# VectorE's share of a two-problem attention kernel: shifted exponential terms made for four key blocks at once, with re-gated weight loads and spread exponentials

## The chip, the cores and the metric

The kernel runs on one core of a Trainium2 chip. The metric is the device time in microseconds (us) of one execution, inputs in HBM to outputs in HBM. The core's engines run side by side, each with its own instruction stream in a fixed order: TensorE (PE), VectorE (DVE), ScalarE (ACT), GpSimd (POOL), and SyncE (SP), which only issues DMAs here. ACT and POOL issue DMAs as well.

## The reference, cut to what matters

Two independent attention problems over 2048 tokens, width 512, 32 heads of width 16. Their outputs stand side by side in the last axis.

```python
# A: four segments of L = 512 tokens, causal softmax inside a segment,
#    plus a linear-attention memory of the segments before
for s in range(4):
    p = softmax(einsum(qs, ks) * scale + mask)        # causal, 512 x 512
    a_dot = p @ vs
    a_mem = (phi(qs) @ M) / (phi(qs) @ z + 1e-6)      # phi(t) = t + 1 if t > 0 else exp(t)
    o = g * a_mem + (1 - g) * a_dot
    M += phi(ks)^T vs;  z += sum(phi(ks))
out_a = concat(o) @ wo

# B: plain softmax attention, 2048 x 2048 per head
out_b = softmax(q @ k^T / 4) @ v @ wo_b
```

Nearly all the work is in problem B: 32 heads times 2048 queries times 2048 keys of scores, each of which needs one exponential.

## The kernel before, in words

**Units.** Problem B is cut into 32 units, each of four heads (`hg` picks which) and 512 queries. Problem A is cut into 32 units likewise, one for each segment and group of four heads. Six A units come first, then B units with the other A units dealt in between. Inside a B unit the scores come in banks: one bank is 128 keys by 512 queries of one head, 64 banks to a unit. Each bank is a matmul into PSUM, an exponential that writes SBUF, and a matmul with the values (called PV here) that adds into the unit's accumulator `acc`.

**Two engines make exponentials.** ACT takes banks in tiles of three and two by turns (`act_tile_b`, L766; `act_tile_a`, L702 for problem A). It reads a PSUM tile `s_ps` and writes the SBUF tile `pT`. DVE takes up to 22 of a unit's 64 banks, one bank at a time, by bit arithmetic: `dve_bank` (L818) reads the bank `d_ps` from PSUM, adds a constant and keeps the maximum with zero, and writes it as int16. Read as fp16, those bits are a coarse power of two. Two further terms, made by adding a constant to the first in int16 (`dve_adds`, L784), and three scaled copies of the values (`VD`, made by POOL at L635) turn it into a good exponential. So one DVE bank needs one instruction on PSUM, a share of two shifted terms in SBUF, and three PV matmuls. The first term and its two shifts lie in a tile `pD` of `PDB` buffers. In the kernel before, such a tile holds two banks and there are five tiles.

**The order of the work is written by a planner.** While the program is built, `fast_path` keeps a model clock for each engine in `c` (`c["t"]` for TensorE, `c["act"]`, `c["dve"]`, `c["gp"]`), with a cost for every operation (`act_cost`, `dve_cost`, `gp_do`). Its main loop (L1021) decides at each model time what TensorE does next: an ACT tile of scores, a DVE bank, PV matmuls (`flush`), a chore, or filler matmuls on zeros (`zeros`, L907) that keep TensorE busy. The choice fixes the order in which all engines' instructions stand. It also shifts banks from DVE's list `dl` to ACT's list `al` when DVE falls behind (`pick`). At run time only that order and the semaphores remain.

**Chores** are the projections (K, Q and V of both problems), the memory products, and the output projections. Each fills a `d_ps` bank through `d_job` and is emptied by DVE (`evac`). PSUM has two `d_ps` banks, shared with the DVE exponentials. A chore starts when its `due` position is reached and its condition (`ok`) holds; for the first projections the condition is a model time by which the weights ought to have landed (`WA_AT`, `WB_AT`, `XB_AT`).

**Loads.** Tokens of A's first segment and a quarter of `wk_a` and `wq_a` come first, half on SP's queue and half on ACT's. `load_rest_a` issues `wv_a` and the rest of `wk_a` and `wq_a` on ACT's queue. `load_b` issues problem B's loads on SP's queue: token transposes in four pieces, then the weights between them.

**phi(K).** For each of four K tiles of a segment, `phi_k` issues a DMA transpose and later an exponential on ACT (L403, tile `ek`) with three POOL operations (L405, L406, L407). The four exponentials of the first segment are all held until the model time `PHI_AT`.

**Tiles named below.** `tT` (two buffers) takes the transposed accumulator in `finalize`, `aT` (one buffer) takes the transposed memory product in `chore_am`, `OT` takes a pair's finished output before the output projection, `QT_a` and `QT_b` hold the masked queries of a pair of units (made by POOL at L353).

Of the kernel before, what the change touches and what calls it, by code (L numbers as in the profile page):

```python
# [41 lines left out]
def fast_path(ctx, tc, nc, A_x, A_wq, A_wk, A_wv, A_wo, A_beta, B_x, B_wqkv, B_wo, out, flag):  # L42
# [8 lines left out]
    pool = lambda name, bufs=1, **k: ctx.enter_context(tc.tile_pool(name=name, bufs=bufs, **k))  # L51
    const = pool("const")
    sb_ = pool("sb")
    PDB, PTB = 5, 4
    QTB = dict(a=2, b=3)
    SCAP, DBANKS = (3, 2), 2
    ps_s = pool("ps_s", 1, space=PSUM)
    ps_d = pool("ps_d", DBANKS, space=PSUM)
# [3 lines left out]
    def wview(w):  # L62
        return w.rearrange("(cc p) n -> p cc n", p=P)
# [101 lines left out]

    def load_rest_a():

        nc.scalar.dma_start(out=wv_a[:], in_=wview(A_wv))
        nc.scalar.dma_start(out=wk_a[:, :, P:], in_=wview(A_wk)[:, :, P:])
        nc.scalar.dma_start(out=wq_a[:, :, P:], in_=wview(A_wq)[:, :, P:])  # L170

# [15 lines left out]
        nc.sync.dma_start(out=wo_a[:], in_=wview(A_wo))  # L187
        nc.sync.dma_start(out=wo_b[:], in_=wview(B_wo))

    WA_AT = dict(v=6500, k=8500, q=10000)  # L190
    XB_AT, WB_AT = (10000, 18000, 23500, 28000), dict(k=13500, v=16000, q=21000)
    PHI_AT = 31000


# [47 lines left out]
    def d_when():  # L242
        return dbank[dcount[0] % DBANKS]
# [29 lines left out]
    def dve_cost(n, rate=1.09):  # L273
        return 75.0 + rate * n
# [97 lines left out]
    def d_job(fill, evac, halves=True):  # L372

        bank = d_bank()
        c["t"] = max(c["t"], d_when())
        if not halves or room_of[0] >= 4 * MM + DR:
            fill(bank, range(4))
            evac(bank)
            return
        n = dcount[0]  # L380
        dbank[n % DBANKS] = 1e18
        dcount[0] += 1
        fill(bank, range(2))

        def rest():
            fill(bank, range(2, 4))
            slot.append(n)
            evac(bank)
        second.append(rest)

    xT_uses, xT_made = {}, {}
# [4 lines left out]
    def phi_k(s, rt):  # L396

        kn = phik_t[(s, rt)] = sb_.tile([P, 4, P], BF16, name="phik", tag="xin", bufs=4)
        nc.sync.dma_start_transpose(out=kn[:], in_=KT_at[(s, rt)][:])

        def more():
            e = sb_.tile([P, 4, P], BF16, name="ek", tag="e", bufs=2)
            nc.scalar.activation(e[:], kn[:], ACT.Exp)  # L403
            act_do(act_cost(512) + 100, c["t"])
            nc.gpsimd.tensor_scalar(e[:], e[:], 1.0, 0.0, ALU.min, ALU.max)  # L405
            nc.gpsimd.tensor_scalar(kn[:], kn[:], 3e38, 0.0, ALU.min, ALU.max)  # L406
            nc.gpsimd.tensor_tensor(kn[:], kn[:], e[:], op=ALU.add)  # L407
            gp_do(1024, c["act"] + LAT)
            gp_do(512, 0, 2.1)
            phik_at[s] = c["gp"] + LAT  # L410
            phik_n[s] = phik_n.get(s, 0) + 1
        at(max(c["dve"] + 12000, PHI_AT), more)

    def chore_k(k, s, rt):
        def evac(bank):
# [77 lines left out]
    def chore_am(u):  # L493
        def fill(bank, _):
            quad(bank, mbds[(u["c"] - 1) % 2][:, u["hg"], :, :].rearrange("p j w -> p (j w)"),
                 PHQ[(u["c"], u["rt"])][0][:], True, True)

        def evac(bank):
            aT = sb_.tile([P, 16, 32], F32, name="aT", tag="aT", bufs=1)
            nc.vector.transpose(aT[:].rearrange("p c d -> p (c d)"), bank)  # L500
            d_done(dve_do(dve_cost(512), c["t"] + LAT))
            r2 = sb_.tile([P, 16, 1], F32, name="r2", tag="r2", bufs=2)
            nc.vector.tensor_scalar(r2[:], aT[:, :, DH:DH + 1], 1e-6, None, ALU.add)
            nc.vector.reciprocal(r2[:], r2[:])  # L504
            dve_do(400, 0)
            tM = sb_.tile([P, 16, DH], F32, name="tM", tag="tM", bufs=2)
            nc.gpsimd.tensor_tensor(tM[:], aT[:, :, 0:DH], r2[:].to_broadcast([P, 16, DH]), op=ALU.mult)  # L507
            gp_do(256, c["dve"] + LAT, 2.1)
            aT_at[0] = c["gp"]
            u["am"] = tM  # L510
        d_job(fill, evac, False)
# [261 lines left out]
                                 ready=sfree[sl] + 100, cnt=cnt, v=("b", kb)))  # L773
        return [j for _, j in banks]

    pd_open = dict(tile=None, n=0, add=None)

    def dve_adds():

        if pd_open["add"] is not None:  # L780
            tile, n, ready, ents, _ = pd_open["add"]
            pd_open["add"] = None
            for k in range(1, NT):
                nc.vector.tensor_scalar(tile[:, k, 0:n, :], tile[:, 0, 0:n, :], EXP_D[k], None, ALU.add)  # L784
                dve_do(dve_cost(512 * n, 0.32), ready + 120)
                for e in ents[k]:
                    e["ready"] = c["dve"] + LAT

    def has_keys(u, kb):
        return k_ready.get(("b", kb // 4, u["rt"]), 1e18) <= c["t"]  # L790
# [7 lines left out]
    def dve_bank(u, j=None):  # L798

        if j is None:  # L800
            j = dve_head(u)
        e = [x for x in u["dl"] if x[1] == j and has_keys(u, x[0])][0]
        u["dl"].remove(e)
        kb, j, slot = e
        bank = d_bank()
        c["t"] = max(c["t"], d_when())
        nc.tensor.matmul(bank, KT_b[32 * j:32 * j + 32, u["rt"], kb * P:(kb + 1) * P],  # L807
                         qslice(u)[32 * j:32 * j + 32, :], start=True, stop=True,
                         tile_position=(32 * j, 0), skip_group_check=True)
        pe(MM, "row", j)  # L810
        if pd_open["tile"] is None:
            pd_open["tile"] = sb_.tile([P, NT, 2, 512], I16, name="pD", tag="pD", bufs=PDB)
            pd_open["n"] = 0
            pd_open["ents"] = [[] for _ in range(NT)]
            pd_open["cnt"] = dict(n=2 * NT, kind=dve_out)
            dve_out[0] += 1
        pd, n = pd_open["tile"], pd_open["n"]
        nc.vector.tensor_scalar(pd[:, 0, n, :], bank, EXP_B, 0.0, ALU.add, ALU.max)  # L818
        d_done(dve_do(dve_cost(512), c["t"] + LAT))
        dve_adds()  # L820
        o = VW * slot
        for k in range(NT):
            e = dict(j=j, c0=0, lhsT=VD_t[u["i"]][:, k, o:o + 32], rhs=pd[:, k, n, :].bitcast(F16),
                     ready=c["dve"] + LAT if k == 0 else 1e15, cnt=pd_open["cnt"], v=("b", kb))
            u["pvq"].append(e)
            pd_open["ents"][k].append(e)
        pd_open["n"] += 1
        pd_open["u"] = u
        if pd_open["n"] == 2:
            pd_open["add"] = (pd, 2, c["dve"], pd_open["ents"], u)  # L830
            pd_open["tile"] = None
        dve_end(u)

    def dve_close():

        if pd_open["tile"] is not None:
            pd_open["cnt"]["n"] -= NT
            pd_open["add"] = (pd_open["tile"], pd_open["n"], c["dve"], pd_open["ents"], pd_open["u"])
            pd_open["tile"] = None
        dve_adds()  # L840

    def dve_end(u):

        if not u["dl"] and (pd_open["tile"] is not None or pd_open["add"] is not None):
            dve_close()

    def exhausted(u):
# [2 lines left out]
    def finalize(u, last):  # L850
# [28 lines left out]
            eng.tensor_tensor(dst, src, u["am"][:].rearrange("p (t c) d -> p c t d", t=2), op=ALU.add)  # L879
        if u["par"] == 1:  # L880
            def turn():
                OT = sb_.tile([P, 8, 32, 2], BF16, name="OT", tag=f"OT_{u['k']}", bufs=5)
                nc.vector.transpose(OT[:].rearrange("p c r t -> p (c r t)").bitcast(F32),
                                    tN_t[key][:].rearrange("p c f t -> p (c f t)").bitcast(F32))
                dve_do(dve_cost(256), 0)
                OT_t[key] = OT
                if u["rt"] == 3 and not last:
                    for sbl in range(4):
                        chore(0, lambda sbl=sbl: chore_out(u["k"], u["c"], sbl), due=prog[0] + 6000 + 4000 * sbl)
                    order_chores()  # L890
            if last:
                turn()
            else:
                at(max(c["dve"], c["gp"]) + 300, turn)
# [55 lines left out]
    for n in range(2):  # L950
        bank = d_bank(BF16)
        fill_xT(bank, (2 * n, 2 * n + 1))
        (nc.scalar.copy if n == 0 else nc.vector.tensor_copy)(
            xt0.rearrange("p c (i s) -> p i c s", s=P)[:, 2 * n:2 * n + 2], bank.rearrange("p (n c s) -> p n c s", n=2, c=4))
        if n == 0:
            load_rest_a()
    (_, pq), (_, pk) = s_tile(), s_tile()
    warm_up(2)
    proj(pq[:, 0, :], range(4), wq_a[:], rsl(0), xt0)
# [61 lines left out]
    while True:  # L1021
# [95 lines left out]
                quiet = False  # L1117
        else:
            quiet = False
        if quiet and pd_open["add"] is not None and pd_open["add"][4] is not u:  # L1120
            pass
        elif (pd_open["add"] is not None or pd_open["tile"] is not None) and du is None and c["dve"] + 300 <= t:
            dve_close()
            continue
        elif pd_open["add"] is not None and c["dve"] + 400 <= t:
            dve_adds()
            continue
        if act_now is not None and du is not None and not due and t + 300 < dwhen <= c["act"] - LATE - 300:

# [66 lines left out]
            wake.append(acc_free[0])  # L1196
        wake += [max(e["ready"], v_ready.get(e["v"], 0)) for e in u["pvq"] if e["ready"] < 1e14]
        wake += list(k_ready.values())[-8:]
        if pd_open["add"] is not None or pd_open["tile"] is not None:
            wake.append(c["dve"] + 401)  # L1200
        if later:
            wake.append(later[0][0])
# [426 lines left out]
```

## Time and profile before

| what | value |
|---|---|
| median of three runs | 907.24 us (904.89 to 907.76) |
| the profiled execution | 907.63 us, of which the span of the profile 905.9 us |
| ACT busy | 841.8 us (93% of the span), 786 instructions |
| PE busy | 794.2 us (88%), 10207 matmuls |
| DVE busy | 787.1 us (87%), 1596 instructions |
| POOL busy | 389.7 us (43%), 779 instructions |
| DVE exponential banks | 586, mean 674 ns (L818) |
| DVE shifted terms | 606 instructions, 566 of them 128x1024, mean 490 ns (L784) |
| ACT exponential tiles of B | 596, mean 1244 ns (L766) |

How to read it: busy time is the time in which an engine had an instruction running, not the time for which it was needed. A row of a group gives the line, the engine, the operation, output and input by the program's names, the count, the busy time and the mean of one, and after the bar the idle time just before such instructions with what ended it. Means include the overlap of neighbouring instructions, so a group's busy time can be less than count times mean. Filler matmuls count as busy.

### The profile page before, as it was taken

The numbers are of one execution on the slowest core, as the hardware profiler recorded it, in microseconds if no ns is written. First come the engines' busy times: TensorE is split into PE (matmuls) and PEld (weight loads), VectorE is DVE, ScalarE is ACT, GpSimd is POOL, SyncE is SP. The second block draws the span as 40 slices with busy tenths as digits, with TensorE's granted clock in tenths as the row PEclk, the third lists the DMA queues.
The fourth block names the chain that finished last, engine by engine and source line by source line (L and its number), as shares of the span: only waits on it lengthen the run. The fifth ranks groups of instructions, "written<-read, shape, count | busy, mean of one in ns | idle before, by whom it ended". The sixth has DMA issues, their size and how long they took to land.

```text
span 905.9 us, 24540 instructions
## 1 busy us (share of the span) xinstructions
PE 794.2 (88%) x10207; PEld 276.7 (31%) x10207; DVE 787.1 (87%) x1596; ACT 841.8 (93%) x786; POOL 389.7 (43%) x779
## 2 busy tenths in 40 slices
PE   7988889989899988899888988889988988988895
PEld 3322233332333322332223323323322332233232
DVE  3546888899999899978999999998899899999984
ACT  5789999999999999999999999999999999999994
POOL 4944424365342255633541554435441533354330
PEclk9999999998999999998999999999999999999997
DMA  8701000000000020010000000100000000000000
GB/s 175 147 2 30 1 3 13 19 9 1 1 8 20 7 31 2 1 31 2 7 2 13 19 2 1 31 2 1 25 2 1 25 3 1 2 2 1 1 25 29
DMA packets 31802, 15.83 MB, mean 17 GB/s; under 512 B 22976, under 2 KB 31680, under 8 KB 31680
## 3 DMA queue, kind: packets, MB, share of 16 engines
q1 hardware_dynamic: 28864, 12.19, 6.4%
q10 hardware_dynamic: 2688, 1.97, 0.7%
q8 instruction: 81, 1.33, 0.6%
q14 instruction: 41, 0.34, 0.1%
q0 software_dynamic: 128, 0.00, 0.0%
HBM read 4.72 MB, written 4.19 MB: 10 GB/s over the span
## 4 chain that ended last, share of the span: by engine, by line
PE 29%; ACT 27%; DVE 27%; issue 10%; POOL 6%; DMA 1%; ACTq 0%; DVEq 0%; POOLq 0%
ACT pT L766 24%; DVE pD L818 11%; PE acc L924 10%; DVE pD L784 9%; PE d_ps L334 7%; PE s_ps L761 6%; DVE tT L855 2%; ACT pT L702 2%; PE s_ps L692 2%; PE d_ps L807 2%; POOL pT L713 2%; PE acc L907 1%; DMA wk_a<-in_A_wk_dram 1%; DVE RA L858 1%; POOL VD L635 1%
## 5 line engine op out<-in xcount | busy, mean ns | idle before, releaser
L766 ACT ACTIVATE pT<-s_ps 128x1536 bf16<-128x1536 f32 (+2 forms) x596 | 675.5, 1244 | 28.1 <-PE d_ps L807 13.2
L818 DVE TENSOR_SCALAR pD<-d_ps 128x512 int16<-128x512 f32 x586 | 379.4, 674 | 20.6 <-PE d_ps L807 18.7
L761 PE MATMUL s_ps<-QT_b,KT_b 32*128 32x512 bf16 x1462 | 233.9, 389 | 52.1 <-ACT pT L766 45.3
L784 DVE TENSOR_SCALAR pD<-pD 128x1024 int16<-128x1024 int16 (+1 forms) x606 | 265.6, 480 | 0.5
L924 PE MATMUL acc<-pD,VD 128*32 128x512 f16 x1758 | 224.3, 389 | 4.6 <-DVE tT L855 4.2
L807 PE MATMUL d_ps<-QT_b,KT_b 32*128 32x512 bf16 x586 | 209.8, 384 | 18.7 <-DVE pD L818 12.8
L924 PE MATMUL acc<-pT,VP_b 128*32 128x512 bf16 x1462 | 223.3, 388 | 0.1
L713 POOL TENSOR_SCALAR_AFFINE_SELECT pT<-pT 128x512 bf16<-128x512 bf16 (+3 forms) x192 | 95.5, 516 | 190.5 <-ACT pT L702 178.4
L702 ACT ACTIVATE pT<-s_ps 128x1024 bf16<-128x1024 f32 (+1 forms) x128 | 138.4, 1145 | 12.7 <-PE s_ps L692 10.5
L761 PEld LDWEIGHTS <-KT_b 32*128 32x128 bf16 x1462 | 71.5, 91 | 245.2 <-issue 233.3
L907 PE MATMUL acc<-ident,zero 128*32 128x256 bf16 (+1 forms) x1700 | 100.1, 292 | 3.9 <-DVE tT L855 3.7
L924 PEld LDWEIGHTS <-VD 128*32 128x32 bf16 x1758 | 62.7, 96 | 71.7 <-issue 52.4
L635 POOL TENSOR_SCALAR VD<-VP_b 128x288 bf16<-128x288 bf16 x192 | 73.9, 385 | 13.5
L924 PEld LDWEIGHTS <-VP_b 128*32 128x32 bf16 x1462 | 61.0, 96 | 47.3 <-issue 31.1
L692 PE MATMUL s_ps<-QT_a,KT_a 32*128 32x384 bf16 (+3 forms) x512 | 56.8, 301 | 11.8 <-ACT pT L702 5.9
L907 PEld LDWEIGHTS <-zero 128*32 128x32 bf16 x1700 | 40.6, 95 | 83.6 <-issue 79.8
L855 DVE STREAM_TRANSPOSE tT<-acc 128x512 f32<-128x512 f32 x64 | 45.2, 707 | 23.1 <-PE acc L924 21.1
L876 POOL TENSOR_TENSOR tN<-tT,RA 128x256 bf16<-128x256 f32 x31 | 20.4, 656 | 76.3 <-DVE RA L858 76.1
L807 PEld LDWEIGHTS <-KT_b 32*128 32x128 bf16 x586 | 46.8, 91 | 12.7 <-issue 9.6
L924 PE MATMUL acc<-pT,VP_a 128*32 128x256 bf16 (+3 forms) x512 | 39.5, 309 | 3.5 <-POOL pT L713 3.0
L507 POOL TENSOR_TENSOR tM<-aT,r 128x256 f32<-128x256 f32 x24 | 15.5, 648 | 60.0 <-DVE r L504 59.8
L353 POOL TENSOR_SCALAR QT_b<-qc,mq 128x512 bf16<-128x512 bf16 x32 | 25.3, 801 | 36.0 <-DVE qc L445 35.8
(111 smaller groups left out, 623.8 us busy)
## 6 DMA issues: line engine op xcount, KB each, us to landing
out_dram<-osb SPq DMA_DIRECT2D x30, 128.0 KB, 1.7
wv_a<-in_A_wv_dram ACTq DMA_DIRECT2D x1, 512.0 KB, 8.6
wk_b<-in_B_wqkv_dram SPq DMA_DIRECT2D x1, 512.0 KB, 6.7
wv_b<-in_B_wqkv_dram SPq DMA_DIRECT2D x1, 512.0 KB, 7.6
wq_b<-in_B_wqkv_dram SPq DMA_DIRECT2D x1, 512.0 KB, 4.9
wo_a<-in_A_wo_dram SPq DMA_DIRECT2D x1, 512.0 KB, 4.5
wo_b<-in_B_wo_dram SPq DMA_DIRECT2D x1, 512.0 KB, 6.7
wk_a<-in_A_wk_dram ACTq DMA_DIRECT2D x1, 384.0 KB, 9.3
```

Source lines behind the costliest of these rows:

```text
L334: nc.tensor.matmul(bank[32 * j:32 * j + 32, :], lhsT[:, 32 * j:32 * j + 32], rhs, start=start, stop=stop, tile_position=(0, 32 * j), skip_ ...
L635: mul = lambda dst, src: nc.gpsimd.tensor_scalar(dst, src, EXP_C[k], 1.0, ALU.mult, ALU.mult)
L692: nc.tensor.matmul(pt[:, b, col:col + w], kt[32 * j:32 * j + 32, kbl * P:(kbl + 1) * P], q[32 * j:32 * j + 32, P * kbl:512], start=(r == 0 ...
L702: nc.scalar.activation(pT[:].rearrange("p b n -> p (b n)")[:, 0:n], pt[:].rearrange("p b n -> p (b n)")[:, 0:n], ACT.Exp, scale=0.25)
L713: nc.gpsimd.affine_select(out=blk, in_=blk, compare_op=ALU.is_ge, fill=0.0, base=0, pattern=[[0, e - b], [0, w // P], [1, P]], channel_mul ...
L761: nc.tensor.matmul(pt[:, b, :], KT_b[32 * j:32 * j + 32, u["rt"], kb * P:(kb + 1) * P], q[32 * j:32 * j + 32, :], start=True, stop=True, t ...
L766: nc.scalar.activation(pT[:, 0:n, :], pt[:, 0:n, :], ACT.Exp, scale=1.0 / (LOG2E * 1024.0))
L784: nc.vector.tensor_scalar(tile[:, k, 0:n, :], tile[:, 0, 0:n, :], EXP_D[k], None, ALU.add)
L807: nc.tensor.matmul(bank, KT_b[32 * j:32 * j + 32, u["rt"], kb * P:(kb + 1) * P], qslice(u)[32 * j:32 * j + 32, :], start=True, stop=True, ...
L818: nc.vector.tensor_scalar(pd[:, 0, n, :], bank, EXP_B, 0.0, ALU.add, ALU.max)
L907: nc.tensor.matmul(bank[32 * j:32 * j + 32, 0:w].rearrange("p (n q) -> p n q", q=P), zero[:, 0:32], ident[:].unsqueeze(1).to_broadcast([P, ...
L924: nc.tensor.matmul(u["acc"][32 * j:32 * j + 32, e["c0"]:512], e["lhsT"], e["rhs"], start=(j not in u["started"]), stop=False, tile_positio ...
```

## The change

The edits, with what each does:

- The `pD` tile holds `PDN` = 4 banks instead of 2, and there are 3 such tiles instead of 5. A shifted term is made by one instruction over 128x2048 instead of two over 128x1024.
- The two shifted terms of a full tile are queued (`pd_open["add"]` is now a list) and given out one at a time (`dve_add`), one behind each following bank, instead of both together. Before a projection is emptied, `d_job` gives out one more when the model's DVE clock stands before the time at which the projection is ready (`last`). The planner's cost of such an instruction is changed as well.
- `load_rest_a` moves behind both halves of the first token transposes. It first has DVE write one element of each target, so that the three loads wait for DVE; `wv_a` goes on SP's queue, `wk_a` and `wq_a` stay on ACT's. The model times of landing are changed to go with it.
- The exponentials of phi(K) of the first segment get model times 3500 ns apart.
- `QT_b` has 2 buffers instead of 3, `OT` 4 instead of 5, and `aT` shares the two buffers of `tT` instead of having its own.

```diff
-    PDB, PTB = 5, 4
-    QTB = dict(a=2, b=3)
+    PDB, PDN, PTB = 3, 4, 4
+    QTB = dict(a=2, b=2)
...
     def load_rest_a():
-        nc.scalar.dma_start(out=wv_a[:], in_=wview(A_wv))
+        for w in (wv_a[:, 0, 0:1], wk_a[:, 0, P:P + 1], wq_a[:, 0, P:P + 1]):
+            nc.vector.memset(w, 0.0)
+        nc.sync.dma_start(out=wv_a[:], in_=wview(A_wv))
         nc.scalar.dma_start(out=wk_a[:, :, P:], in_=wview(A_wk)[:, :, P:])
         nc.scalar.dma_start(out=wq_a[:, :, P:], in_=wview(A_wq)[:, :, P:])
...
-    WA_AT = dict(v=6500, k=8500, q=10000)
-    XB_AT, WB_AT = (10000, 18000, 23500, 28000), dict(k=13500, v=16000, q=21000)
+    WA_AT = dict(v=7500, k=9000, q=10500)
+    XB_AT, WB_AT = (11500, 19500, 24000, 27500), dict(k=13000, v=14500, q=21000)
...
+        def last(bank):
+            if pd_open["add"] and c["dve"] + 300 < c["t"] + LAT:
+                dve_add()
+            evac(bank)
         if not halves or room_of[0] >= 4 * MM + DR:
             fill(bank, range(4))
-            evac(bank)
+            last(bank)
...
-        at(max(c["dve"] + 12000, PHI_AT), more)
+        at(max(c["dve"] + 12000, PHI_AT + 3500 * rt), more)
...
-            aT = sb_.tile([P, 16, 32], F32, name="aT", tag="aT", bufs=1)
+            aT = sb_.tile([P, 16, 32], F32, name="aT", tag="tT", bufs=2)
...
-    pd_open = dict(tile=None, n=0, add=None)
-    def dve_adds():
-        if pd_open["add"] is not None:
-            tile, n, ready, ents, _ = pd_open["add"]
-            pd_open["add"] = None
-            for k in range(1, NT):
-                nc.vector.tensor_scalar(tile[:, k, 0:n, :], tile[:, 0, 0:n, :], EXP_D[k], None, ALU.add)
-                dve_do(dve_cost(512 * n, 0.32), ready + 120)
-                for e in ents[k]:
-                    e["ready"] = c["dve"] + LAT
+    pd_open = dict(tile=None, n=0, add=[])
+    def dve_add():
+        if pd_open["add"]:
+            k, tile, n, ready, ents, _ = pd_open["add"].pop(0)
+            nc.vector.tensor_scalar(tile[:, k, 0:n, :], tile[:, 0, 0:n, :], EXP_D[k], None, ALU.add)
+            dve_do(150.0 + 0.3 * 512 * n, ready + 120)
+            for e in ents:
+                e["ready"] = c["dve"] + LAT
+    def dve_full(u):
+        pd_open["add"] += [(k, pd_open["tile"], pd_open["n"], c["dve"], pd_open["ents"][k], u) for k in range(1, NT)]
+        pd_open["tile"] = None
...
-            pd_open["tile"] = sb_.tile([P, NT, 2, 512], I16, name="pD", tag="pD", bufs=PDB)
+            pd_open["tile"] = sb_.tile([P, NT, PDN, 512], I16, name="pD", tag="pD", bufs=PDB)
...
-        if pd_open["n"] == 2:
-            pd_open["add"] = (pd, 2, c["dve"], pd_open["ents"], u)
-            pd_open["tile"] = None
+        if pd_open["n"] == PDN:
+            dve_full(u)
...
     def dve_close():
         if pd_open["tile"] is not None:
-            pd_open["cnt"]["n"] -= NT
-            pd_open["add"] = (pd_open["tile"], pd_open["n"], c["dve"], pd_open["ents"], pd_open["u"])
-            pd_open["tile"] = None
-        dve_adds()
+            pd_open["cnt"]["n"] -= NT * (PDN - pd_open["n"])
+            dve_full(pd_open["u"])
+        while pd_open["add"]:
+            dve_add()
...
-                OT = sb_.tile([P, 8, 32, 2], BF16, name="OT", tag=f"OT_{u['k']}", bufs=5)
+                OT = sb_.tile([P, 8, 32, 2], BF16, name="OT", tag=f"OT_{u['k']}", bufs=4)
...
-        if n == 0:
-            load_rest_a()
+    load_rest_a()
```

## The prediction

> **What bounds the kernel now.** I read the busy totals first, then busy time by stage, then the waits of ACT and of TensorE in the long middle stage, then the groups of DVE. Busy time by stage (each row: length, then busy time of PE, PEld, DVE, ACT, POOL):
>
> ```profile
> PE 794.2 (88%) x10207; PEld 276.7 (31%) x10207; DVE 787.1 (87%) x1596; ACT 841.8 (93%) x786; POOL 389.7 (43%) x779
> ...
> 0.00:75.00 75.00, 64.19 (x884) 24.24 (x885) 34.13 (x81) 55.29 (x57) 45.70 (x112) 0.98 0.49 98
> 75.00:875.00 800.00, 710.19 (x9062) 244.58 (x9061) 733.75 (x1475) 769.15 (x715) 336.04 (x664) 0.99 0.04 10
> 875.00:905.90 30.90, 19.80 (x264) 7.83 (x261) 19.27 (x41) 17.34 (x17) 7.95 (x5) 0.84 0.08 25
> ```
>
> ACT is the nearest to its limit. Its idle time is 905.9 - 841.8 = 64.1 us: 19.7 in the first 75 us, 30.85 in the middle 800, 13.6 at the end. A change that leaves ACT's work alone can gain at most what it takes out of these. DVE is second: 66 us idle in the middle. The two meet at TensorE, which feeds both in one fixed order. The waits in the middle stage, of ACT and then of TensorE:
>
> ```profile
> ACT pT L766 <- PE d_ps L807: 11.9, 30, 1.0
> ACT pT L766 <- PE s_ps L761: 10.2, 19, 1.5
> ACT pT L702 <- PE s_ps L692: 3.0, 10, 0.4
> ACT pT L702 <- PE d_ps L807: 1.2, 5, 0.4
> ...
> PE s_ps L761 <- ACT pT L766: 43.6, 120, 0.8
> PE d_ps L807 <- DVE pD L818: 12.5, 30, 1.0
> PE acc L924 <- DVE tT L855: 4.2, 9, 1.1
> PE acc L907 <- DVE tT L855: 3.7, 10, 0.7
> PE d_ps L334 <- DVE pD L818: 3.6, 8, 1.0
> ```
>
> TensorE waits for ACT most (43.6 us): there ACT is the bound and DVE costs nothing. In some 60 other places TensorE stands before a bank or an accumulator that DVE has not emptied (12.5 + 4.2 + 3.7 + 3.6 = 24 us), and the ACT tile queued behind in TensorE's order comes late. ACT's waits behind `d_ps L807`, 11.9 + 1.2 = 13.1 us, bear that mark most plainly. So a quicker DVE is worth a part of 27 us, not its own saving.
>
> **The shifted terms.**
>
> ```profile
> L818 DVE TENSOR_SCALAR pD<-d_ps 128x512 int16<-128x512 f32 x586 | 379.4, 674 | 20.6 <-PE d_ps L807 18.7
> L784 DVE TENSOR_SCALAR pD<-pD 128x1024 int16<-128x1024 int16 x566 | 254.4, 490 | 0.5
> L784 DVE TENSOR_SCALAR pD<-pD 128x512 int16<-128x512 int16 x40 | 12.5, 352 | 0.0
> ```
>
> 512 more elements cost 490 - 352 = 138 ns, so 128x2048 is estimated at 490 + 2 x 138 = 766 ns and 128x1536 at 628. In the instruction lists of the two built programs the terms go from 566 + 40 instructions to 276 of 2048, 16 of 1536, 4 of 1024 and 22 of 512. Before: 566 x 490 + 40 x 352 = 291.4 us of durations; the page shows 265.6 busy, so neighbours overlap by 43 ns each. After: 276 x 766 + 16 x 628 + 4 x 490 + 22 x 352 = 231.2, less 318 x 43 ns, 217.6 us. Saved: 48.0 us. DVE gets five more banks (591), 5 x 647 ns (379.4/586) = 3.2. Net 44.8 us, 5.7% of DVE's busy time.
>
> ACT's list changes little: eight fewer tiles of three banks (1475 ns), eight more of two (1050 ns), three more of one (656 ns): -11.8 + 8.4 + 2.0 = **-1.4 us** of ACT work. So the planner does not hand the freed DVE time to more banks. The planner's own costs say why: a bank with its terms was priced at 633 + 403 = 1036 ns and took about 1100 (647 + 265.6/586); it is now priced at 633 + 382 = 1015 and should take 647 + 217.6/591 = 1015. ACT stays priced low (1379 against 1475 ns). Before, both engines ran late against the written order; now only ACT should. I therefore expect TensorE to wait more for ACT and less for DVE.
>
> Worth in the middle: of the 13.1 us marked by `d_ps L807` I take three quarters, **-10 us**. The bounds: +4 (the whole order is written anew, and new gaps can open) and -22 (ACT idle falling everywhere to the 0.27 us in 25 of the best stretch of that length leaves 8.6 of 30.85). As a second reading, the chain that ended last holds 9.1% of `DVE pD L784`, 82 us; 18% of that (48.0/265.6) is 15 us.
>
> One rule speaks against long SBUF instructions on DVE. The trace first: of the 566 shifted terms, 361 met no POOL instruction and took 414 ns; the 205 that did took 622. The Trainium skill, "SBUF — State Buffer", section "SBUF: two separate sides", says that DVE in a two-port mode and GpSimd share a port pair as an exclusive lock for the whole instruction, and the other blocks fully. By the row, the lock is in the 766. By the rule, a term's wait depends on how often it starts, not on its length: 414 + 2 x 131 = 676 (the lone 512 took 283) plus 0.36 x 208 = 75, or 751 ns, so 4 us less in all. POOL pays: each term now shuts it out for 0.68 us instead of 0.41. With terms running 24% of the time (217.6/906) instead of 29%, and a mean wait of half a term, its 779 instructions wait 779 x (0.24 x 0.34 - 0.29 x 0.21), about 16 us, more; POOL holds 6% of the chain, so I take +1 us. Its cover is its 57% idle time.
>
> **Loads.** ACT's first exponential waits for the K projection, and that for `wk_a`:
>
> ```profile
> PE s_ps L334 <- DMA wk_a<-in_A_wk_dram: 1.5, 1, 1.5
> 5.65 3.54 ACTq L170 DMA_DIRECT2D wq_a<-in_A_wq_dram  x1
> 8.87 1.05 PE L334 MATMUL s_ps<-xT_a,wk_a 128*32 128x512 bf16 x16 [1.47 <-DMA wk_a<-in_A_wk_dram]
> 26.70 4.20 ACT L702 ACTIVATE pT<-s_ps 128x1280 bf16<-128x1280 f32 x4 [3.42 <-PE s_ps L692]
> 46.27 0.63 ACT L403 ACTIVATE ek<-phik 128x512 bf16<-128x512 bf16 x1 [3.11 <-POOL phik L407]
> ```
>
> The first quarter of `wk_a` took 7.1 us on ACT's queue; that of `wq_a`, equally large, took 4.2 on SP's. The large loads were issued at 4.66 right behind it. Gated behind DVE's copy (which ended at 6.20) they leave at about 6.4. If they were what delayed it, 1.47 us is gained, since TensorE then follows `wq_a` directly; if not, nothing. The Trainium skill, "DMA: Bandwidth & Descriptors", section "Issuing engines are not separate DMA queues", says that DMAs from all issuers run on the same 16 engines and a second issuer saves only issue time. By it the move of `wv_a` to SP is worth nothing; by the row, ACT's queue stuck for 3.54 us in the third issue, it frees ACT. ACT had nothing else before 9.96, so I take half the gate: **-0.7**. The price is `wv_a`: 8.6 us from issue before, so by 15.0 instead of 13.2 at worst; the V projection waits up to 1.8 us with ACT tiles queued behind. I take **+0.5**. On SP `wv_a` stands ahead of the first B transpose, but leaves before it is due (8.23), so its issue delays nothing; sharing the bandwidth, the transpose may land later. B's K and V are not needed before 50 us.
>
> **POOL and phi(K).** ACT's 3.42 us wait is for masks that POOL made behind two causal selects (0.89 us). In the new lists the masks stand first: **-0.9**. The 3.11 us wait is the third phi(K) exponential, whose tile (two buffers) POOL still held; 3500 ns apart, with score tiles between, POOL's 2.4 us for each is covered: **-3.0**. Should the transposed K land late, the first one waits, up to about 2 us.
>
> **Smaller buffers**, taken at 0 each: a `QT_b` pair is wanted once in two B units, and its projection is due 9 us ahead; without that cover ACT would wait some 3 us (16 matmuls 1.05, copy 0.68, masks 1.36). `OT` comes round again after four pairs, long after its output projection. `tT` and `aT` together are taken 88 times, one each 10 us, and POOL holds one for 2 to 3 us; where POOL is behind, DVE waits about 1 us.
>
> **The sum** on the profiled execution: -1.4 - 10 + 1 - 0.7 + 0.5 - 0.9 - 3.0 = -14.5, against its 907.63 us (span 905.9 and 1.7 around it): 893 us. The median shown, 907.24, is 0.4 us lower; I leave that in the rounding.
>
> **The rivals.**
> - *Freed DVE time is only idle time.* For it: over 5 us stretches of the middle, ACT idles 0.19 us where DVE is full and 0.1 to 0.25 where it has room, so a full DVE may not be the cause. Against: the 24 us of TensorE's waits for DVE. Then only the front, POOL's 1 us and ACT's work count: 907.6 - 4.1 + 1 - 1.4, about 903 us.
> - *The written order fits the chip now, and most gaps close.* DVE priced right takes out all gaps but ACT's own step: -22 instead of -10, 881 us.
> - *Slower: the end of a unit.* The last two terms of a unit now come as up to 2 x 766 instead of 2 x 490 ns after its last bank, and the only `acc` is free only after the PV matmuls on them. That is 0.55 us at each of 32 B units, 17.7 us. Before, DVE already sat 19.1 us in the middle until the last PV matmul (`tT` from `acc`). It decides when ACT's four `pT` buffers of each size are full at that moment; then the time is 907.6 - 4.1 + 17.7 - 1.4, about 920 us. Against: TensorE hardly waited for L784 (0.2 us).
> - *The change doesn't do what it says*, the terms costing in proportion: excluded by 490 against 352 ns for double the size.
>
> **How the numbers follow.** 0.3% (2.7 us) is about what a measurement of this kernel can tell from no change. Main case, middle gain 4 to 16 us: 0.57, 887 to 899 us. Gaps close: 0.12, 876 to 887. Freed time idle: 0.17, 899 to 906, of it 0.05 within 0.3%. Slower by the units' ends or a worse order: 0.14, of it 0.02 within. Faster 0.81, same 0.07, slower 0.12. A range of 880 to 907 leaves out about 0.06 below and 0.13 above.
>
> **What would show it.** Terms of 2048 at 750 to 770 ns, about 276 of them; DVE busy near 742 us; ACT busy within 3 us of 840; `PE d_ps L807 <- DVE pD L818` under 6 us and `PE s_ps L761 <- ACT` above 45; middle ACT idle near 20 us; no 3 us wait at `ek`. Wrong if DVE's busy time falls so and ACT's middle idle stays at 30, or if `PE acc` waits for the shifted terms.

## The result and the profile after

The changed kernel takes 895.59 us (median of 4 runs, 893.92 to 896.06), against 907.50 us for the kernel before beside it (904.89 to 908.79): a ratio of 0.9869, 95% interval 0.9843 to 0.9895. The profiled execution took 896.06 us, with a span of 894.3 us, 11.6 us less than before's 905.9.

Busy totals of the page (PEld: TensorE's weight loads), then by stage the length, busy time of PE, PEld, DVE, ACT and POOL, the granted share of the TensorE clock, the DMA engines' busy share and GB/s:

```profile
PE 798.8 (89%) x10093; PEld 278.2 (31%) x10093; DVE 747.4 (84%) x1316; ACT 837.3 (94%) x789; POOL 406.1 (45%) x779
...
0.00:75.00 75.00, 67.72 (x939) 27.13 (x939) 36.52 (x88) 60.03 (x61) 49.50 (x123) 0.98 0.49 99
75.00:863.30 788.30, 712.16 (x8897) 243.86 (x8895) 692.50 (x1196) 761.09 (x714) 350.73 (x654) 0.99 0.04 10
863.30:894.30 31.00, 18.93 (x263) 7.21 (x259) 18.38 (x34) 16.14 (x16) 5.84 (x4) 0.91 0.08 26
```

ACT's idle time is stage length minus ACT's busy time. It went from 19.7 to 15.0 us at the front, from 30.85 to 27.2 in the middle, and from 13.6 to 14.9 at the end. ACT's busy time fell by 4.5 us. Together: 4.7 + 3.6 - 1.3 + 4.5 = 11.5, which is the change of the span. So the middle, where DVE was relieved of 41 us (733.75 to 692.50), gave back only 3.6 us of ACT's idle time.

The groups of the shifted terms, and what ACT and then TensorE waited for in the middle (total us, times, longest; the last line is the kernel before):

```profile
L828 DVE TENSOR_SCALAR pD<-d_ps 128x512 int16<-128x512 f32 x591 | 384.6, 676 | 34.9 <-PE d_ps L817 32.6 <-PE s_ps L700 0.3
L790 DVE TENSOR_SCALAR pD<-pD 128x2048 int16<-128x2048 int16 x276 | 201.9, 738 | 0.7
...
ACT pT L774 <- PE d_ps L817: 11.1, 20, 1.8
ACT pT L774 <- PE s_ps L769: 8.3, 19, 1.7
...
PE s_ps L769 <- ACT pT L774: 35.8, 107, 0.7
PE acc L933 <- POOL pT L721: 7.4, 13, 1.0
PE d_ps L817 <- DVE pD L828: 7.1, 26, 0.6
...
PE acc L924 <- POOL pT L713: 1.1, 3, 0.6
```

The lengths came out close to what was worked out: 276 terms of 2048 elements at 738 ns. TensorE's wait for DVE to empty a bank fell from 12.5 to 7.1 us. A new wait stands above it: PV matmuls of problem A that wait for POOL's causal select (L721; L713 in the kernel before, where it was 1.1 us). I put each gap of ACT of at least 100 ns in the middle to the last wait of TensorE in the 3 us ahead of it. By that sorting, gaps behind TensorE's wait for DVE's bank fell from 6.2 to 2.8 us, and gaps behind its wait for the select rose from 0.6 to 7.6 us. The chain that ended last, before and after, says the same:

```profile
PE 29%; ACT 27%; DVE 27%; issue 10%; POOL 6%; DMA 1%; ACTq 0%; DVEq 0%; POOLq 0%
...
ACT 33%; PE 25%; issue 15%; POOL 13%; DVE 12%; DMA 1%; ACTq 0%; SPq 0%; DVEq 0%; POOLq 0%
```

DVE's share fell from 27% to 12%, and POOL's doubled from 6% to 13%.

### The profile page after: what moved, and what is told of

Same layout as the page of the kernel before. It is cut to its first block, busy times and chain, and to the rows that moved or that the text cites. A ratio compares the mean times of both kernels' runs of the same rounds, so it can differ in the third digit from the quotient of the medians.

```text
span 894.3 us, 24040 instructions
## 1 busy us (share of the span) xinstructions
PE 798.8 (89%) x10093; PEld 278.2 (31%) x10093; DVE 747.4 (84%) x1316; ACT 837.3 (94%) x789; POOL 406.1 (45%) x779
## 4 chain that ended last, share of the span: by engine, by line
ACT 33%; PE 25%; issue 15%; POOL 13%; DVE 12%; DMA 1%; ACTq 0%; SPq 0%; DVEq 0%; POOLq 0%
ACT pT L774 27%; PE acc L933 8%; PE d_ps L336 6%; ACT pT L710 5%; PE s_ps L769 5%; DVE pD L828 5%; POOL pT L721 4%; DVE pD L790 3%; POOL VD L643 2%; PE d_ps L817 2%; PE s_ps L700 2%; DVE tT L864 1%; PE acc L916 1%; POOL tN L885 1%; POOL QT_a L355 1%
## 5 line engine op out<-in xcount | busy, mean ns | idle before, releaser
L774 ACT ACTIVATE pT<-s_ps 128x1536 bf16<-128x1536 f32 (+2 forms) x599 | 671.7, 1240 | 23.9 <-PE d_ps L817 11.1
L828 DVE TENSOR_SCALAR pD<-d_ps 128x512 int16<-128x512 f32 x591 | 384.6, 676 | 34.9 <-PE d_ps L817 32.6
L721 POOL TENSOR_SCALAR_AFFINE_SELECT pT<-pT 128x512 bf16<-128x512 bf16 (+3 forms) x192 | 100.9, 545 | 263.3 <-ACT pT L710 261.7
L933 PE MATMUL acc<-pD,VD 128*32 128x512 f16 x1773 | 217.5, 388 | 2.5 <-DVE tT L864 2.2
L790 DVE TENSOR_SCALAR pD<-pD 128x2048 int16<-128x2048 int16 (+3 forms) x318 | 217.0, 696 | 1.0
L933 PE MATMUL acc<-pT,VP_b 128*32 128x512 bf16 x1457 | 211.7, 386 | 0.0
L769 PEld LDWEIGHTS <-KT_b 32*128 32x128 bf16 x1457 | 74.0, 91 | 241.4 <-issue 227.3
L710 ACT ACTIVATE pT<-s_ps 128x1280 bf16<-128x1280 f32 (+1 forms) x128 | 138.7, 1159 | 9.0 <-PE s_ps L700 6.8
L643 POOL TENSOR_SCALAR VD<-VP_b 128x288 bf16<-128x288 bf16 x192 | 76.4, 398 | 13.6
L864 DVE STREAM_TRANSPOSE tT<-acc 128x512 f32<-128x512 f32 x64 | 45.4, 709 | 33.9 <-PE acc L933 23.9
L700 PE MATMUL s_ps<-QT_a,KT_a 32*128 32x512 bf16 (+3 forms) x512 | 56.9, 300 | 11.1 <-ACT pT L774 5.0
L817 PEld LDWEIGHTS <-KT_b 32*128 32x128 bf16 x591 | 47.7, 91 | 19.5 <-issue 17.0
L700 PEld LDWEIGHTS <-KT_a 32*128 32x128 bf16 x512 | 19.2, 91 | 65.1 <-issue 58.8
```

The lines of the kernel that those rows point to most:

```text
L643: mul = lambda dst, src: nc.gpsimd.tensor_scalar(dst, src, EXP_C[k], 1.0, ALU.mult, ALU.mult)
L700: nc.tensor.matmul(pt[:, b, col:col + w], kt[32 * j:32 * j + 32, kbl * P:(kbl + 1) * P], q[32 * j:32 * j + 32, P * kbl:512], start=(r == 0 ...
L710: nc.scalar.activation(pT[:].rearrange("p b n -> p (b n)")[:, 0:n], pt[:].rearrange("p b n -> p (b n)")[:, 0:n], ACT.Exp, scale=0.25)
L721: nc.gpsimd.affine_select(out=blk, in_=blk, compare_op=ALU.is_ge, fill=0.0, base=0, pattern=[[0, e - b], [0, w // P], [1, P]], channel_mul ...
L769: nc.tensor.matmul(pt[:, b, :], KT_b[32 * j:32 * j + 32, u["rt"], kb * P:(kb + 1) * P], q[32 * j:32 * j + 32, :], start=True, stop=True, t ...
L774: nc.scalar.activation(pT[:, 0:n, :], pt[:, 0:n, :], ACT.Exp, scale=1.0 / (LOG2E * 1024.0))
```

## The experiments

Theory: the gain has two sources, the loads and phi(K) at the front and DVE's relief in the middle, and part of the second is handed back to POOL. Rivals: DVE's freed time is idle; the load and phi edits do nothing; or any new order moves the time by chance. Each ratio below is to the kernel before on the same chip, with its 95% interval.

### The three parts alone (e1, e2, e3)

The first takes the changed kernel and puts the loads, their model times and phi(K) back:

```diff
-    WA_AT = dict(v=7500, k=9000, q=10500)
+    WA_AT = dict(v=6500, k=8500, q=10000)
...
-        nc.sync.dma_start(out=wv_a[:], in_=wview(A_wv))
+        nc.scalar.dma_start(out=wv_a[:], in_=wview(A_wv))
...
-        at(max(c["dve"] + 12000, PHI_AT + 3500 * rt), more)
+        at(max(c["dve"] + 12000, PHI_AT), more)
```

> The changed kernel with everything ahead of the attention as it was before: loads, their due times, the place of the rest-of-A loads and the phi(K) exponentials are those of the kernel before; the 2048-element terms, the way they are placed and the buffer counts are those of the changed kernel. Theory (two sources: some 4.5 us come from the first 75 us, the other 7 from VectorE's relief later): 7 us faster than before, 900 to 901 us, ratio 0.992; ACT busy near 838, DVE busy near 747, the 3 us ACT wait at the second phi(K) exponential still there. Rival (only the front pays; freed VectorE time turns idle): 906 to 908 us, ratio 0.999 or more. Rival (only the terms pay, the front edits are noise): 895 to 897, ratio 0.987.

The other two take the kernel before and make one of these edits each. e2 is the last line above the other way round; e3 is the load edits with all their model times.

> The kernel before with one edit, the four phi(K) exponentials of a segment due 3500 ns apart. Theory: it removes ACT's wait of 3.1 us at the second of them and nothing else, so 3 us faster, 904 to 905 us, ratio 0.9965. Rival (the order that follows is what matters, each reshuffle moves the time by some microseconds either way): anything from 900 to 912 with ACT's idle time changed after the first 75 us rather than in them. Rival (the wait moves to the next instruction): 907 to 908, ratio 1.000.

> The kernel before with the load edits alone: gated weight loads on the SyncE queue, due times of A and B work, the rest of A's weights issued after both transposed banks. Theory: the first exponential starts 1.9 us later as in the changed kernel (12.9 us in place of 11.0) and most of that is won back by the masks ahead of the causal selects and earlier B loads, so the sum lies between -1.5 and +1 us: 906 to 908.5, ratio 0.998 to 1.001. Rival (the loads carry the front's gain): 902 to 904, ratio 0.995. Rival (the later start is paid in full): 909 to 910, ratio 1.002.

| kernel | median us | ratio to before |
|---|---|---|
| e1, terms and buffers alone | 900.47 | 0.9925 (0.9901 to 0.9949) |
| e2, phi(K) apart alone | 904.02 | 0.9959 (0.9930 to 0.9987) |
| e3, loads alone | 904.64 | 0.9964 (0.9943 to 0.9985) |

At 907.5 us these are gains of 6.8, 3.7 and 3.3 us, 13.8 in all against 11.9 for the whole change; the intervals, some 2 to 2.5 us each way, allow the sum. So each of the three kernels is faster, and "only the front" and "only the terms" both fall. The terms gave the 7 us expected of them, and phi(K) its 3 us: in e2 ACT's idle time fell in the first 75 us, from 19.7 to 17.3, and not behind them. The loads gave more than the -1.5 to +1 expected. ACT's timeline of e3 (start, length, what, in brackets the idle time before it) shows where ACT waited less:

```profile
24.30 4.20 ACT L704 ACTIVATE pT<-s_ps 128x1280 bf16<-128x1280 f32 x4 [1.08 <-PE s_ps L694]
...
43.91 0.63 ACT L405 ACTIVATE ek<-phik 128x512 bf16<-128x512 bf16 x1 [1.00 <-POOL phik L409]
```

The 3.42 us wait for POOL's masks is 1.08 here, though some comes back earlier (3.14 us at 21.50, where before had 0.51). The 3.11 us wait at the third `ek` is 1.00, although phi(K) was left alone: the loads changed the order around it. ACT's idle time in the first 75 us is 15.8 us against 19.7, but 1.6 of that comes back at the end, and the profiled execution of e3 is only 1.5 us shorter than before's. How much of e3's 3.3 us the loads themselves brought stays open; the granted clock (see the next section) is a rival for most of it.

### Two blocks instead of four (e4), three (e8)

```diff
-    PDB, PDN, PTB = 3, 4, 4
+    PDB, PDN, PTB = 6, 2, 4
```

> The changed kernel with tiles of two key blocks (six buffers of half the size, so the same memory) and its terms still given out one at a time wherever VectorE waits. VectorE gets back about 276 instructions and some 40 us of busy time (747 to about 786); the hold on the port that it shares with POOL gets shorter. Theory (VectorE's relief pays, POOL's longer ops take some of it back): PE's waits for POOL's causal selects fall from 7.4 us to under 3, but PE's waits for VectorE's pD rise from 7 to over 10, and the sum is 2 to 4 us slower than the changed kernel: 897.5 to 899.5 (ratio to before 0.990). Rival (placement alone pays, not the length of a term): as the changed kernel within 1 us, 895 to 896.5 (0.987). Rival (the port is the main loss): 889 to 892 (0.981). Rival (the length alone pays): 903 or more (0.995).

e8 has `PDB, PDN, PTB = 4, 3, 4`.

> The changed kernel with tiles of three key blocks, four buffers (the same memory): terms of 1536 elements. Theory (time rises with the length of the term, through POOL and through the blocks that wait for a tile to fill): between e4 and the changed kernel, 889 to 893, ratio 0.981; PE's waits for POOL 3 to 5 us. Rival (only the order that comes out counts, with no trend over the size): outside 887 to 896.

Measured: e4 886.66 us, 0.9771 (0.9734 to 0.9808); e8 885.56 us, 0.9789 (0.9754 to 0.9825). By their ratios and medians both are 7 to 10 us faster than the changed kernel, and they cannot be told from each other. My theory had e4 slower, and it came out faster than all four expectations. e8's median lies below its theory's 889 to 893, where its rival (only the order that comes out counts) had put it. In the order that the change writes, the part that its title names, four blocks at once, costs time. From e4's page and its waits in the middle:

```profile
PE 773.9 (87%) x10177; PEld 275.5 (31%) x10177; DVE 766.6 (87%) x1586; ACT 839.3 (95%) x788; POOL 394.8 (45%) x779
...
PE s_ps L769 <- ACT pT L774: 59.7, 151, 0.8
PE d_ps L817 <- DVE pD L828: 5.5, 17, 0.9
...
PE acc L933 <- POOL pT L721: 1.7, 4, 0.7
```

DVE has 19 us more to do, and TensorE waits for it less than in the changed kernel, for POOL hardly at all, and much more for ACT, the engine nearest to its limit. e8 has 3.6 us of waits for the select, between the two, but is no slower for it; so time does not rise evenly with the length of the term. Fewer blocks to a tile also mean more tiles (six of two, four of three, for three of four), and a tile fills sooner; these were not varied apart.

### The same order with the terms halved (e5)

If POOL suffers from the length of a term, cutting each term in two must help POOL, with all else in place:

```diff
-            nc.vector.tensor_scalar(tile[:, k, 0:n, :], tile[:, 0, 0:n, :], EXP_D[k], None, ALU.add)
+            for h in range(0, n, 2):
+                w = min(n, h + 2)
+                nc.vector.tensor_scalar(tile[:, k, h:w, :], tile[:, 0, h:w, :], EXP_D[k], None, ALU.add)
```

> The changed kernel with every 2048-element term issued as two 1024-element ones, one behind the other, at the same places: the order of all other instructions and their plan are unchanged. It adds some 276 instructions and some 276 x (2 x 455 - 738) = 47 us of VectorE busy time (747 to about 795), and halves each hold of the port that VectorE and POOL share. Theory (the length of the hold is what costs: it makes POOL's causal selects late): PE's waits for POOL fall from 7.4 us to under 3, selects that meet a term drop from 911 to about 750 ns, time 888 to 892, ratio 0.980. Rival (the placement of four-block tiles is at fault, not the port): POOL waits stay at 6 or more and VectorE's added work makes later banks wait: 896 to 903, ratio 0.987 to 0.995.

Measured: 910.29 us, 1.0027 (0.9998 to 1.0057): some 14 us slower than the changed kernel, outside both expectations. TensorE's waits in its middle:

```profile
PE s_ps L769 <- ACT pT L774: 25.2, 80, 0.7
PE d_ps L819 <- DVE pD L830: 18.1, 42, 1.3
...
PE acc L935 <- POOL pT L721: 1.3, 5, 0.4
```

Both halves of the answer are in these lines. The waits for POOL went from 7.4 to 1.3 us, and a 512-wide select that met a term took 763 ns instead of 911 (639 alone): the length of the hold does make POOL late. But the 37 us that DVE needs more (784.5 busy) were not in the plan, and TensorE's waits for DVE's banks went from 7.1 to 18.1 us. In a fixed order, 37 us of DVE time cost about 14 us, even with POOL relieved. So "freed DVE time is idle" falls, and the number of terms matters after all; e4, with as many, isn't slowed by them, presumably because its order was planned with them.

### One at a time or both together (e6)

e6 is e4 with both terms of a tile issued in a row (`while` for `if` in `dve_add`); where its expectation counts three terms, a tile has two.

> The two-block kernel (e4) with all three terms of a tile issued in a row, as in the kernel before, in place of one at each wait; the front, the other buffers and the tile count are e4's. Theory (what pays in e4 is that a projection or a new bank waits for one term and not for three, so a bank slot comes free up to 900 ns sooner): 898 to 902 us, ratio 0.991, about what the loads and phi edits alone give; PE's waits for pD back near 12 us. Rival (more tiles, six in place of five, or the tail of the change pays): as e4, 885 to 889, ratio 0.977.

Measured: 896.83 us, 0.9895 (0.9859 to 0.9932), a little faster than the theory's 898 to 902 and far from the rival's 889 at most. Giving the terms out one at a time is worth some 10 us here (0.9895 against 0.9771). Half of that is not a wait but work: the planner took ten more banks from DVE (571 for e4's 581), and ACT's busy time rose from 839.3 to 844.5 us. TensorE's wait for DVE's banks in the middle rose from 5.5 to 8.7 us, where "near 12" was expected.

### POOL's price in the planner (e7, e10)

The planner prices a 512-wide select at 638 ns. It measured 671 on average before and 724 after. One number raises it to 738:

```diff
-        c["gp"] = max(c["gp"], ready) + 100.0 + rate * n
+        c["gp"] = max(c["gp"], ready) + 200.0 + rate * n
```

> The changed kernel with one number of the planner changed: an operation of POOL is taken as 200 ns + its elements in place of 100 ns, which gives 738 ns for a 512-wide causal select (measured 724 on average) in place of 638. Theory (the planner sends PE to results that POOL hasn't made yet because terms twice as long delay POOL): PE's waits for POOL's selects fall from 7.4 us to under 3, ACT's idle time in the middle by some 4 us, time 890 to 893, ratio 0.982. Rival (the wait moves on to another instruction, since PE has nothing else ready): POOL waits gone but 895 to 898, ratio 0.987. Rival (a different order, worse by luck): 899 or more.

The same edit in the kernel before:

> The kernel before with POOL's operations taken as 200 ns + elements, as in e7. Theory (POOL's underprice cost nothing before, when PE waited for its selects for 1.1 us only, and came to cost with the longer terms): within 3 us of before, 904 to 909, ratio 0.997 to 1.002. Rival (the price helps whatever the terms' length, so e7's gain has nothing to do with the change): 892 to 897, ratio 0.985.

Measured: e7 881.48 us, 0.9732 (0.9700 to 0.9764), faster than expected; e10 908.38 us, 1.0025 (1.0003 to 1.0048), as the theory had it. The price brings nothing before the change, and 12 us (by the ratios) to 14 us (by the medians) after it. e7's middle stage and its waits:

```profile
75.00:848.90 773.90, 696.54 (x8864) 238.54 (x8861) 686.56 (x1187) 757.97 (x711) 351.92 (x652) 0.99 0.04 10
...
PE s_ps L769 <- ACT pT L774: 47.4, 131, 0.8
...
PE d_ps L817 <- DVE pD L828: 4.1, 13, 0.7
PE acc L933 <- DVE tT L864: 2.9, 7, 0.9
```

No line for POOL's select is among TensorE's waits in the middle any more. ACT's idle time in the middle is 773.90 - 757.97 = 15.9 us, against 27.2. The terms are as long as in the changed kernel; only 11 of the 64 full-width selects met one, instead of 20, and the plan, which counts on a select later, places its PV matmuls later. The selects of the changed kernel and of e7:

```profile
L721 POOL TENSOR_SCALAR_AFFINE_SELECT pT<-pT 128x512 bf16<-128x512 bf16 x64 | 46.1, 724 | 4.9 <-ACT pT L710 3.5
...
L721 POOL TENSOR_SCALAR_AFFINE_SELECT pT<-pT 128x512 bf16<-128x512 bf16 x64 | 41.0, 644 | 7.3 <-ACT pT L710 5.8
```

In e7 itself a select took 644 ns, near the old price of 638. So 738 is no truer there; it works as a margin. That fewer selects met a term is nothing that the price aims at. Among the kernels below, e12 has 17 that met one and took 825 ns on average, and no wait for a select either, so the margin is enough without it. e7 is the fastest kernel run, and it beats both of those compared.

### Does an honest price alone do it? (e9)

The change also brings the planner's price of a term near to what it takes (764 ns for 2048 elements, measured 738), where the kernel before had 403 for a measured 490. So I gave the kernel before the right price:

```diff
-                dve_do(dve_cost(512 * n, 0.32), ready + 120)
+                dve_do(175.0 + 0.3 * 512 * n, ready + 120)
```

> The kernel before with one number of the planner changed: a 1024-element term is taken as 482 ns (measured 490) in place of 403. The three terms in a row were some 260 ns underpriced. Theory (a good part of what the terms brought is that the plan now knows how long VectorE is busy, since the halved terms, which take unplanned time, cost 15 us): 3 to 6 us faster than before, 901 to 904, ratio 0.995; PE's waits for pD fall from 12 us to under 9. Rival (the price is unimportant, only fewer and single terms pay): 906 to 909, ratio 1.000.

(A tile has two such terms, so the two were some 160 to 175 ns too cheap.) Measured: 912.33 us, 1.0084 (1.0052 to 1.0116): slower than either side expected. Its busy line, its middle stage and its groups:

```profile
PE 789.4 (87%) x10291; PEld 275.1 (30%) x10291; DVE 760.7 (84%) x1534; ACT 853.5 (94%) x803; POOL 387.0 (43%) x779
...
75.00:876.20 801.20, 706.90 (x9133) 243.41 (x9132) 706.51 (x1413) 780.85 (x732) 333.76 (x665) 1.00 0.04 10
...
L818 DVE TENSOR_SCALAR pD<-d_ps 128x512 int16<-128x512 f32 x554 | 360.3, 675 | 32.9 <-PE d_ps L807 30.1 <-PE s_ps L761 0.7
```

ACT's middle idle time fell from 30.85 to 20.35 us, as an order that fits the chip should make it (though TensorE's waits for DVE's banks stayed at 11.9 us, where under 9 was expected). But the planner, seeing what DVE really costs, gave DVE only 554 banks instead of 586, and ACT's busy time rose by 11.7 us. An honest price alone closes gaps and pays for them with ACT's work. The change lowered the cost to where the honest price left DVE its banks (591).

### Both cures together (e11, e12)

> The two-block kernel (e4) with POOL's price of e7. Theory (two cures of the same wait, so they don't add; e4 has 1.7 us of waits for selects left): 883 to 887, ratio 0.976. Rival (they act in different ways and add): 872 to 876, ratio 0.964.

> The three-block kernel (e8) with POOL's price of e7. Theory (two cures of the same wait; e8 has 3.6 us of waits for selects left): 880 to 884, ratio 0.973, like e7. Rival (they add): 870 to 875, ratio 0.962. Rival (order luck): over 888.

Measured: e11 887.73 us, 0.9788 (0.9762 to 0.9814), no better than e4; e12 882.64 us, 0.9741 (0.9715 to 0.9767), like e7. Shorter terms and POOL's price do not add as the rivals had it (872 to 876 and 870 to 875), which fits that they cure the same wait. With that wait out of the way, four blocks are no worse than three; two (e11) lie 0.6% behind, with intervals that just touch, so that small order I leave open.

## Why the prediction was right, point by point

893.0 us was forecast and 895.59 came; the sum of -14.5 us stands against -11.6 on the profiled executions. That it came so near is in part luck: the middle fell 5.4 us short of the -9 forecast for it (POOL's +1 included) and the end lost 1.3, while ACT's busy time gave 3.1 more than forecast and the front 0.6 more.

- **The terms' length.** 766 ns was taken for 2048 elements, and 738 measured. Terms that met no POOL instruction took 682 ns (172 of them), those that did 831 (104). The reading by the Trainium skill ("SBUF — State Buffer", section "SBUF: two separate sides": an exclusive lock, from which the prediction took that a term's wait does not grow with its length) gave 751 and was nearer than the row's slope. The group's busy time was 217.0 us for a forecast of 217.6. DVE's whole busy time fell by 39.7 us instead of 44.8: the banks took 5.2 more instead of 3.2, and the other groups about 3.7 more.
- **The middle, -10 us, was the mis-sized term.** ACT's idle time there fell by 3.6. The mechanism was right: TensorE's wait for DVE's banks fell (7.1 us; under 6 was forecast), and the e5 run shows that DVE's time costs when it is not there. But I looked for 20 us of idle time and for over 45 us of TensorE waiting for ACT, and 27.2 and 35.8 came. e7 shows both as forecast, or better (15.9 and 47.4).
- **POOL's +1 us was the main reason.** The prediction said that the longer hold would let POOL's instructions wait some 16 us more; POOL's busy time rose by 16.4. The failed step came next: it covered this with POOL's 57% idle time. An average hides that a select has PV matmuls waiting, in an order written with 638 ns in mind. The wait came to 7.4 us on TensorE, 7.6 us of ACT's gaps, and e7's price brought 12 to 14 us of time. By the sorting above, e7 has nothing left of the 7.6; the next point has most of the rest of its 11.3 us in the middle. The same section of the skill names the price (the other side blocks fully); only the waits of TensorE tell where it is paid.
- **The granted clock was in no term.** The traces record it as full or half, the half in stretches of 3.4 us or more. In the middle the half clock held for 23.9 us before, 17.1 after, 10.2 in e7 and none in e8, and ACT idled 4.6, 4.8, 2.2 and 0 us inside these stretches. Repeated executions of one kernel differ with it: over all runs listed, 0.001 more of the mean granted clock goes with 0.5 us less time. The means are 0.982 to 0.984 for the kernel before, 0.987 for the changed kernel, 0.991 for e7, 0.992 for e4 and e8, 0.978 for e5 and 0.987 for e3. By that slope, an estimate, some 2 us of the change's 11.9 go with the clock, 2 to 3 of e7's further 12 to 14, 4 to 5 of the 14 us by which e5 fell behind, and most of e3's 3.3. It need not be a cause of its own: in the 3.4 us ahead of each half-clock stretch in the middle, TensorE was busy 57 to 87% of the time before and after, against 89 and 90% on average, so its waits may bring the half clock on. No run varies the two apart.
- **ACT's work, -1.4 us,** measured -4.5. The instruction counts were those of the forecast. The lengths of ACT's instructions added up to 931.0 us against 927.2 before, so no work went away: more neighbours overlap (664 pairs against 639), and busy time is their union. Part of what the forecast booked as less idle time in the middle showed up as less busy time; ACT's idle time in the middle and its busy time together fell by 8.1 us, against the -10.4 forecast for these three terms.
- **The front, -4.1 us by its four terms,** measured -4.7 of ACT's idle time. phi(K) was right at -3.0 (e2: 3.7). So were the masks at -0.9: before, ACT waited 0.51 us at 21.50 and 3.42 at 26.70, after 2.21 at 22.98 and 0.75 at 25.45, which is 0.97 us less. The gate on `wk_a`, -0.7, can't be confirmed. In this profile the first exponential even came 1.9 us later, at 12.93 instead of 11.04; the waits of 0.54 and 1.39 us that stood behind it before are gone, so that the late start cost nothing in the end. Some 1.6 us of the 1.9 goes with the clock: the 32 first matmuls ran at half of it (last section) and took 3.54 us from first to last, against 1.91 in e3. But e1, with the old loads, has this exponential at 12.73, and e3, with the new ones, at 10.51. Over all fourteen profiles the old loads (5) give 9.61 to 12.73, mean 10.93, and the new ones (9) give 9.14 to 12.93, mean 10.67; the three latest, 12.93, 12.73 and 12.14 (e7), are those with the half clock. The +0.5 for `wv_a` did not come: it landed at 13.37 us (13.24 before), and the V projection began at 15.79 without waiting for it.
- **The rivals.** Freed DVE time as idle time (903) falls with e1 and e5. The slow end of a unit (920) fell too: TensorE waited 0.2 us for the shifted terms. That most gaps close (881) did not happen; e7 measured its time, but with 15.9 us of ACT's idle time left in the middle, where this rival had 8.6. That a new order moves the time by chance is not excluded by itself: each kernel is one order, and the intervals are over its repetitions. e10, a new order without a gain to look for, lies some 2 us from before; e2 and e3 are not much larger than that, the terms, e4, e7, e8 and e12 are.
- **The small buffers** taken at nothing were not tried alone; no wait for one of them to come free stands out in the profile after.

## What to carry to other kernels

When an order is written ahead by a cost model, a faster instruction pays only as far as the order leaves room for what it does to the other engines. So after each change set the measured means beside the model's prices, also on the engine that you did not touch and that looks half idle, and try a margin there. Here a longer instruction on DVE in SBUF was bought with POOL's time: look for who waits for POOL before calling that time free. And see what a new price does to the split of the work, since a truer price can close gaps and still lose by moving work to the engine nearest its limit.

## What the runs showed of the hardware that was not expected

- POOL's operations stretch with the length of the term that they meet. A 512-wide select that met one took 730 ns with 1024-element terms in the kernel before and 911 ns with 2048-element ones; alone it took 637 and 639. The 911 is the mean of two groups: nine took 633 to 640 ns and eleven 1070 to 1183, so a select either lost nothing or stood for most of a term. In e7 one of the eleven that met a term took 1091 ns and ten 636 to 640.
- The first load scatters by more than the edit to it. The DMA for the first quarter of `wq_a` left SP's queue at the same 2.14 us in all fourteen profiles, with nothing of the change ahead of it, and landed between 5.30 and 8.37 us.
- The first projections' 16 matmuls took 1.05 us in most profiles, and 1.90 and 1.86 in the one of the changed kernel. The Trainium skill, "TensorE: Matmul & The Clock Gate", "Part 1: The HAM clock gate", gives a cold array half the rate. The traces' clock records agree: the changed kernel has half clock from 8.2 to 11.6 us, and e7 no full clock before 10.8. In all fourteen profiles a matmul of these projections took 376 to 392 ns when it lay wholly inside a stretch recorded at full clock, and 586 to 634 when wholly outside. The waits ahead of them do not sort it: e7 waited 1.18 us and took 1.90, e4 waited 1.85 us and took 1.05.

```profile
8.25 1.90 PE L336 MATMUL s_ps<-xT_a,wq_a 128*32 128x512 bf16 x16 [2.61 <-DMA wq_a<-in_A_wq_dram]
...
7.50 1.90 PE L336 MATMUL s_ps<-xT_a,wq_a 128*32 128x512 bf16 x16 [1.18 <-DMA wq_a<-in_A_wq_dram]
...
7.89 1.05 PE L336 MATMUL s_ps<-xT_a,wq_a 128*32 128x512 bf16 x16 [1.85 <-DMA wq_a<-in_A_wq_dram]
```

The lines are from the changed kernel, e7 and e4.
